# First rows' variance taken ahead of the second rows' statistics, the first weights converted on GpSimd, and transposed rows in four tiles at both ends

## The chip, the cores and the metric

The kernel runs on one core of a Trainium2 chip. The metric is the device time of one execution in microseconds. The core has five engines with queues of their own: TensorE (PE; its weight loads are PEld), VectorE (DVE), ScalarE (ACT), GpSimd (POOL) and SyncE (SP), which only issues transfers here. ACT issues transfers too. The engines run in the order of their queues and meet through semaphores.

## The reference

Two equal layers: sliding-window attention with 32 heads of 20 over 2048 rows of 640 (window 256), and a dense block with a squared ReLU; both have a layernorm ahead and a residual around them.

```
def _A_ref(x, wqkv, wo):
    B, S, D = x.shape                      # 1, 2048, 640
    H = 32; Dh = D // H; W = 256
    qkv = (lambda x, *d: x.transpose(*d))((x @ wqkv).reshape(B, S, 3, H, Dh), 2, 0, 3, 1, 4)
    q, k, v = qkv[0], qkv[1], qkv[2]
    scores = jnp.einsum("bhqd,bhkd->bhqk", q, k) * (Dh ** -0.5)
    idx = jnp.arange(S)
    mask = (idx[:, None] - idx[None, :] >= 0) & (idx[:, None] - idx[None, :] < W)
    scores = jnp.where(mask[None, None], scores, -1e9)
    p = _softmax(scores, axis=-1)
    o = jnp.einsum("bhqk,bhkd->bhqd", p, v)
    return (lambda x, *d: x.transpose(*d))(o, 0, 2, 1, 3).reshape(B, S, D) @ wo

def _B_ref(x, w1, b1, w2, b2):
    h = jnp.einsum("bsd,df->bsf", x, w1) + b1     # 640 -> 1536
    r = jnp.where(h > 0, h, 0)
    return jnp.einsum("bsf,fd->bsd", r * r, w2) + b2

x = x + _A_ref(_layernorm(x), A_wqkv, A_wo);  x = x + _B_ref(_layernorm(x), ...)   # twice
```

## The kernel before

The work is cut into 16 units u: two layers of eight groups, each of 256 rows (two tiles xt of 128 x 640). A unit goes through these stages.

- **Layernorm** (`ln_load`, `layernorm`): two statistics on DVE for each tile of 128 rows (L353), aggregate (L357) and variance (L358), the power -1/2 on GpSimd (L364), the scaling on DVE (L366).
- **Transposes** (`ln_t`, `split_t`): PE turns a tile in five matmuls (L391) into a PSUM tile bb, ACT casts it to a high half in fp16 (L377), DVE makes the low half as the difference (L378). Both halves stand in one tile yT.
- **Three-term products** (`mm3`, L327): each dense product is high x high + high x low + low x high, three matmuls for each of five chunks of the contraction, 15 for a block of 128 columns of q or k. High and low halves of the weights come from `convert`: ACT makes the high half (L259), DVE the low one (L260).
- **q, k** (`stage_qk`): evicted by ACT and DVE (L507, L510) into fp16 halves, then sent through DRAM in another layout (`leave`, L542 to L548). **v** (`stage_v`, L580).
- **Attention** in eight quads of four heads. `max_quad` computes all scores of a quad for their row maxima (L653; L668 for a layer's first group), with DVE reducing them (L633); `max_out` turns the maxima (L721, L726, L727) and `rows_out` sends them as a row qt<-mT that is a further row of the contraction (L689); `exp_quad` computes the scores again with it (L757, L765), ACT takes the exponential into pt (L779), GpSimd masks (L794, L798); `pv_quad` multiplies with v (L828), ot goes out through DRAM (o, L840, L845) and comes back in `load_o` (L904 to L914) as od.
- **Dense rest**: `stage_o` (od x wo), a layernorm, `stage_y` (transposed rows y2, again through `split_t`), `stage_f` (w1, ReLU L1003, square L1007, w2, the sum L1042 and the rows out).

Weights are loaded at the start: wq in seven pieces on SP's queue, `load_wq` (L273), wo in four on ACT's queue (L288, into w_s), w1 and w2 behind them. All stay in SBUF.

The order of the work on each engine is not left to a scheduler. A planner in the kernel keeps a clock `now` for PE and one for each other engine; `post` puts a job with an estimated cost (ns) and a priority into a list, and `pump` emits what can start by the planned clock. `flow` puts the first unit's quads between the dense work of the units ahead as soon as their planned inputs are there; `together` does it for later units. So a changed cost or a new job changes what is emitted behind it on all engines, until the plan falls back into step. `spin` (L341) emits matmuls on a constant tile into nothing: 14 at the start and 7 behind the first transposes. krow[0] (named kt in the profile) is the tile of the first keys, whose constant is set by four memsets of 128x512 (L96); mh are two tiles for the turned maxima, zeroed at L593.

In quarter units (all but a layer's first group) a maxima quad holds four row blocks w of 5 x 64 = 320 key columns, laid one behind the other over PSUM banks of 512 columns; a block that crosses a bank's end is cut into pieces, one matmul each. w stands for the pair j and half i:

```
for w in range(4):
    j, i = divmod(w, 2)
    p, at = 2 * qd + j, 5 * Q * w
    cuts = sorted({0, 5 * Q, *(z - at for z in (512, 1024) if 0 < z - at < 5 * Q)})
```

Of the kernel before, what the change touches and what calls it, by code (L numbers as in the profile page):

```python
# [11 lines left out]
F16 = mybir.dt.float16  # L12
BF16 = mybir.dt.bfloat16
AF = mybir.ActivationFunctionType
ALU = mybir.AluOpType
# [30 lines left out]
def kernel(ctx: ExitStack, tc: tile.TileContext, x, wqkv, wo, w1, b1, w2, b2, out):  # L46
# [50 lines left out]

    for k in range(4):
        set_row(0, k)

# [155 lines left out]

    def convert(st, hi, low, n, load, *deps, prio=2):

        a = post("A", 20 + 0.9 * n, lambda: nc.scalar.activation(hi, st, AF.Copy, scale=WS), load, *deps, prio=prio)  # L259
        return post("D", 30 + 1.04 * n, lambda: nc.vector.scalar_tensor_tensor(low, st, WS, hi, op0=ALU.mult,  # L260
                                                                               op1=ALU.subtract), a, prio=prio)
# [59 lines left out]

    def mm3(acc, lhs, rhs, nk, ns, then=None):

        k, t = 0, 0.0
        for c in range(nk):
            for a, b in ((0, 0), (0, 1), (1, 0)):
                nc.tensor.matmul(acc, lhs(a, c), rhs(b, c), start=(k == 0), stop=(k == 3 * nk - 1))  # L327
# [17 lines left out]

    def layernorm(src, y, *deps, prio=2):

        box = {}

        def stats(i):  # L350
            if i == 0:
                box["st"] = sb.tile([P, 2, 6], F32, name="bst", bufs=2)
            nc.vector.bn_stats(box["st"][:, i, :], src[:, i * HD:(i + 1) * HD])  # L353

        def var():
            box["mv"] = mv = sb.tile([P, 4], F32, name="bmv", bufs=2)
            nc.vector.bn_aggr(mv[:, 0:2], box["st"])  # L357
# [6 lines left out]
        j = post("G", 520, lambda: nc.gpsimd.tensor_tensor(box["mv"][:, 3:4], box["mv"][:, 2:3], neghalf,  # L364
                                                                   op=ALU.pow), j, prio=prio)
        j = post("D", 576, lambda: nc.vector.tensor_scalar(y, src, box["mv"][:, 0:1], box["mv"][:, 3:4],  # L366
                                                           op0=ALU.subtract, op1=ALU.mult), j, prio=prio)
        return j

    def split_t(y, dst, job, made, bb=None):  # L370

# [4 lines left out]
        def out(tr, jobs, c0, n, wait):  # L376
            j = post("A", 170 * n, lambda: nc.scalar.copy(dst[:, 0, c0:c0 + n], tr[:, :n]), wait=wait, prio=0)  # L377
            j = post("D", 170 * n, lambda: nc.vector.tensor_sub(dst[:, 1, c0:c0 + n], tr[:, :n], dst[:, 0, c0:c0 + n]), j,  # L378
                     prio=0)
# [32 lines left out]
    def ln_load(u, *deps, prio=2):  # L412
# [3 lines left out]
        for i in range(2):  # L416
            xt = sb.tile([P, D], F32, name="xt", tag="xt", bufs=2)
            load = dma(lambda xt=xt, i=i: nc.sync.dma_start(xt, xsrc(l, 2 * g + i)), P * D * 4, *deps, prio=min(prio, 1))
            ys.append((xt, layernorm(xt, xt, load, prio=prio)))
        lns[u] = ys  # L420

    def ln_t(u, yT=None):
        ys = lns.pop(u)
        if yT is None:
            yT = sb.tile([P, 2, KC, T], F16, name="yT", tag="yT", bufs=1)
        yTs[u], pre[u] = yT, []
        bb = banks() if u == 0 else (None, None)
        for i in range(2):
            yield from split_t(ys[i][0], yT[:, :, :, i * P:(i + 1) * P], ys[i][1], pre[u], bb[i])

# [24 lines left out]
    def ln_cross(u, *deps):  # L455
# [4 lines left out]
        def dst():  # L460
            yTs[u] = sb.tile([P, 2, KC, T], F16, name="yT", tag="yT", bufs=1)
            return yTs[u]

# [14 lines left out]
    def stage_qk(u, which=(0, 1)):  # L478
# [9 lines left out]
        for j, c0 in order:  # L488
# [33 lines left out]
            for c in range(n):  # L522
                lo = j * D + (c0 + c) * P
                need(wqj[lo // P])
                yield from mm3(acc[:, c, :], lambda a, k: wq_s[:, a, k, lo:lo + P],
                               lambda b, k: yT[:, b, k, :], KC, 109, evict if c == n - 1 else None)

# [39 lines left out]
    def stage_v(u, which=range(4)):  # L567
        yT = yTs[u]
        for i in range(2):
# [3 lines left out]
            for h in range(2):  # L573
# [5 lines left out]
                def out(vt=vt, acc=acc, h=h):  # L579
# [3 lines left out]

                yield from mm3(acc[:, :HD], lambda a, k: yT[:, a, k, i * P:(i + 1) * P],
                               lambda b, k: wq_s[:, b, k, 2 * D + h * HD:2 * D + (h + 1) * HD], KC, 136,
# [5 lines left out]
    mhs = [sb.tile([P, P], F16, name=f"mh{i}") for i in range(2)]  # L591
    for m in mhs:
        nc.vector.memset(m, 0.0)  # L593

# [12 lines left out]
    def by_tiles(pieces):  # L607
# [5 lines left out]
        for _, _, put in sorted(order, key=lambda o: o[:2]):  # L613
            for e in range(2):
                put(e)

    def max_quad(n):
# [19 lines left out]
        if quarters(u):  # L637
            flat = [b.rearrange("p a n -> p (a n)") for b in bb]
            pieces = []
            for w in range(4):  # L640
                j, i = divmod(w, 2)
                p, at = 2 * qd + j, 5 * Q * w
# [16 lines left out]
            now[0] += 763.0  # L659
            for w in range(4):  # L660
# [301 lines left out]
    def y_cross(u):  # L962
        def dst():
            y2s[u] = sb.tile([P, 2, KC, T], F16, name="y2", tag="qd", bufs=1)
            return y2s[u]

# [7 lines left out]
    def stage_y(u, *between):  # L974

        y2s[u] = y2 = sb.tile([P, 2, KC, T], F16, name="y2", tag="qd", bufs=1)
        ypre[u] = []
        bb = banks() if u == NU - 1 else (None, None)
        for i in range(2):
            y, j = ys.pop((u, i))  # L980
            yield from split_t(y, y2[:, :, :, i * P:(i + 1) * P], j, ypre[u], bb[i])
            for g in between[i:i + 1]:
                yield from g

    def stage_f(u, ahead=None):
# [8 lines left out]
        for f0 in range(0, FC, 2):  # L994
# [26 lines left out]
            for f in range(2):  # L1021
                fo = (f0 + f) * P
                need(w1j[f0 + f])
                yield from mm3(acc[:, f, :], lambda a, k: w1_s[:, a, k, fo:fo + P],
                               lambda c, k: y2[:, c, k, :], KC, 109, evict if f else None)
        if ahead is not None:
# [164 lines left out]

    spin(14)
    ln_load(0, prio=0)
    load_wq()
    run(ln_t(0))
    spin(7)
    rate[0] = 250.0
# [86 lines left out]
```

## Time and profile before

| | us |
|---|---|
| median of 3 runs | 1586.17 |
| lowest, highest | 1585.07, 1589.79 |
| the profiled execution, its own time | 1588.33 |
| its span in the trace | 1586.6 |
| granted clock of TensorE, mean over the span | 0.995 |

The span is what the profiler saw between the first and the last instruction; 1.7 us of the profiled execution's time lie around it. In the rows of a timeline the first two numbers are the start and the length in us, then come engine, line, operation, output <- inputs and a count; in brackets stand the idle time of the engine just before and what ended it. Neighbouring instructions of one kind are drawn together (x148). In the rows of windows there are the busy time and the count of each engine, then the granted clock (PEclk, 1.00 is full speed), the share of the DMA engines and GB/s. In the groups by line, the numbers behind the bar are the busy time in us and the mean ns of one.

### The profile page before, as it was taken

To read this page: it belongs to the slowest core of one execution; us is meant where nothing else is said; L and a number is where in the kernel's file an instruction comes from. 1 tells how busy PE (TensorE), PEld (TensorE's weight loads), DVE (VectorE), ACT (ScalarE), POOL (GpSimd) and SP (SyncE) were. 2 spreads that over 40 slices of the span, in tenths; PEclk is the share of its full clock that TensorE was granted. 3 is DMA by queue.
4 is the path that set the end of the run, shared out by engine and by line. 5 is a ranking of instruction groups with operands and counts; after the bars stand their busy time and mean duration, and the time that the engine had idled before them with its cause. 6 is when DMAs were issued, how large, how long until landed. Compare 5 with 4: busy or idle time off the path is not lost. (4 is left out here: it accounts for less than half of the span.)

```text
span 1586.6 us, 52541 instructions
## 1 busy us (share of the span) xinstructions
PE 1558.1 (98%) x21570; PEld 1168.7 (74%) x21570; DVE 984.7 (62%) x3254; ACT 734.3 (46%) x1593; POOL 600.3 (38%) x1291
## 2 busy tenths in 40 slices
PE   8899999999999999999999999999999999999989
PEld 7666777777777777777777777777778777676767
DVE  8776665666756656565566656657665666756532
ACT  4455545444454444535443453444535345354512
POOL 1233534235253443524324252442525325254512
PEclk9998999999999999999999999999999999999999
DMA  9764343362533525354352534535343343431020
GB/s 272 191 181 117 77 107 86 96 131 55 122 87 103 111 57 127 78 124 90 91 132 64 121 87 110 104 70 128 68 125 83 97 111 69 114 87 58 29 67 18
DMA packets 243353, 160.44 MB, mean 101 GB/s; under 512 B 91176, under 2 KB 226856, under 8 KB 243112
## 3 DMA queue, kind: packets, MB, share of 16 engines
q1 hardware_dynamic: 236744, 147.58, 38.8%
q10 hardware_dynamic: 6368, 9.50, 2.1%
q8 instruction: 169, 2.77, 0.7%
q14 instruction: 72, 0.59, 0.1%
HBM read 84.68 MB, written 52.95 MB: 87 GB/s over the span
## 5 line engine op out<-in xcount | busy, mean ns | idle before, releaser
L779 ACT ACTIVATE pt<-bb 128x512 f32<-128x512 f32 (+1 forms) x736 | 376.0, 600 | 227.0 <-PE bb L757 197.8
L633 DVE CUSTOM_DVE_ANT_0 bb<-bb,maskq 128x320 f32<-128x320 f32 x896 | 409.2, 524 | 86.8 <-PE bb L653 74.6
L794 POOL TENSOR_SCALAR_AFFINE_SELECT pt<-pt 128x256 f32<-128x256 f32 x448 | 188.0, 422 | 563.1 <-ACT pt L779 550.3
L327 PE MATMUL acc<-y,w_s 128*128 128x256 f16 x2880 | 328.3, 273 | 2.5 <-ACT y L377 1.4
L327 PE MATMUL acc<-w_s,hh 128*128 128x320 f16 (+1 forms) x2340 | 326.1, 297 | 0.0
L327 PEld LDWEIGHTS <-w_s 128*128 128x128 f16 x2880 | 276.5, 98 | 54.4 <-issue 18.1
L327 PEld LDWEIGHTS <-hh 128*128 128x128 f16 x2340 | 222.1, 98 | 96.8 <-issue 11.5
L327 PEld LDWEIGHTS <-wq_s 128*128 128x128 f16 x2400 | 229.9, 98 | 46.3 <-issue 13.5
L327 PE MATMUL acc<-yT,wq_s 128*128 128x256 f16 x2250 | 258.6, 273 | 2.2 <-DVE qd L510 0.8
L798 POOL TENSOR_SCALAR_AFFINE_SELECT pt<-pt 128x256 f32<-128x256 f32 x512 | 213.7, 439 | 93.0 <-ACT pt L779 91.6
L1013 DVE TENSOR_TENSOR hh<-r,hh 128x256 f16<-128x256 f32 x192 | 95.1, 517 | 208.8 <-ACT hh L1010 201.8
L828 PE MATMUL pv<-pt,vt 128*32 128x128 f32 (+1 forms) x3840 | 190.9, 331 | 1.2 <-POOL pt L798 1.2
L1007 POOL TENSOR_TENSOR r<-r 128x256 f32<-128x256 f32 x192 | 114.2, 615 | 161.2 <-ACT r L1003 158.8
L840 ACT COPY ot<-pv 128x256 f32<-128x256 f32 x128 | 47.7, 373 | 268.8 <-PE pv L828 268.7
L327 PE MATMUL acc<-wo_s,od 128*128 128x320 f16 x960 | 141.7, 303 | 4.8 <-ACT od L911 3.0
L633 DVE DVE_READ_ACCUMULATOR2_ANT mx<- 128x1 f32 x1024 | 145.1, 142 | 0.0
L828 PEld LDWEIGHTS pv<-pt,vt 128*32 128x32 f32 x3840 | 105.4, 110 | 41.7 <-POOL pt L798 6.5
L327 PE MATMUL acc<-wq_s,yT 128*128 128x320 f16 x900 | 132.0, 299 | 1.4 <-DVE y L378 0.9
L327 PEld LDWEIGHTS <-od 128*128 128x128 f16 x960 | 92.1, 99 | 51.0 <-issue 6.4
L1003 ACT ACTIVATE r<-acc,b1s 128x256 f32<-128x256 f32 x192 | 80.7, 472 | 87.7 <-PE acc L327 86.4
L327 PEld LDWEIGHTS <-yT 128*128 128x128 f16 x900 | 85.7, 98 | 39.3 <-issue 6.7
L364 POOL TENSOR_TENSOR bmv<-bmv,neghalf 128x1 f32<-128x1 f32 x64 | 45.5, 717 | 136.1 <-DVE bmv L358 135.7
(95 smaller groups left out, 1226.3 us busy)
## 6 DMA issues: line engine op xcount, KB each, us to landing
qt<-qk SPq DMA_DIRECT2D x30, 480.0 KB
kt<-qk SPq DMA_DIRECT2D x30, 480.0 KB
qk<-qd SPq DMA_DIRECT2D x17, 640.0 KB
o<-ot SPq DMA_DIRECT2D x256, 42.0 KB
od<-o SPq DMA_DIRECT2D x14, 640.0 KB
qk<-yl SPq DMA_DIRECT2D x13, 640.0 KB
qk<-qd SPq DMA_DIRECT2D x17, 320.0 KB
xt<-in_A_x_dram SPq DMA_DIRECT2D x16, 320.0 KB
```

The costliest lines, as they stand in the source:

```text
L327: nc.tensor.matmul(acc, lhs(a, c), rhs(b, c), start=(k == 0), stop=(k == 3 * nk - 1))
L364: j = post("G", 520, lambda: nc.gpsimd.tensor_tensor(box["mv"][:, 3:4], box["mv"][:, 2:3], neghalf, op=ALU.pow), j, prio=prio)
L633: nc.vector.tensor_tensor_reduce(out=v, in0=v, in1=mask, scale=1.0, scalar=-3.0e38, op0=ALU.add, op1=ALU.max, accum_out=accum[e, w]),
L779: nc.scalar.activation(box["pt"][:, :o], bb[e][:, k, :o], AF.Exp, scale=SCALE / (QS * QS))
L794: nc.gpsimd.affine_select(out=m, in_=m, pattern=[[0, 2], [-1, P]], compare_op=ALU.is_gt, fill=0.0, base=0, channel_multiplier=1)
L798: nc.gpsimd.affine_select(out=m, in_=m, pattern=[[0, 2], [1, P]], compare_op=ALU.is_ge, fill=0.0, base=0, channel_multiplier=-1)
L828: nc.tensor.matmul(pv[32 * jj:32 * (jj + 1), q0 * P:(q0 + qn) * P], vf[:, c:c + 32], pj[:, j, :], start=(k == 0), stop=(k == len(steps) - ...
L840: nc.scalar.copy(ot[:, qd % 2], pv)
L1003: nc.scalar.activation(box["r"], acc[:, f, :], AF.Relu, bias=b1s[:, f0 + f:f0 + f + 1], scale=1.0 / (YS * WS))
L1007: nc.gpsimd.tensor_tensor(box["r"], box["r"], box["r"], op=ALU.mult)
L1013: nc.vector.tensor_sub(hh[:, 1, f, :], box["r"], hh[:, 0, f, :])
```

## The change

Five edits.

1. `ln_load` and `layernorm`: for u = 0 the first tile's aggregate and variance are made before the second tile's statistics, and both scalings after both variances.
2. The four memsets of krow[0] and the two of mh go from DVE to GpSimd (`set_first`), posted behind the first unit's transposes.
3. The high half of the first 128 columns of wq is made by GpSimd (`tensor_scalar`) in place of ACT.
4. The transposed rows of u = 0 and u = 15 stand in four tiles in place of one (high chunks 0 to 2, high 3 and 4, low 0 to 2, low 3 and 4), so that a matmul waits for its own piece. The first q block of u = 0 and the first w1 block of u = 15 take their three terms one after the other over all five chunks (`whole`), not chunk by chunk: for u = 0 high x high, high weights x low rows, low weights x high rows; for u = 15 the last two the other way round.
5. The order of the row blocks in a maxima quad is `TURN`: (0,1), (0,0), (1,0), (1,1). With the bank ends at 512 and 1024 the pieces of one pair of heads that lay in two banks become one: 36 matmuls for a quad in place of 38, in 112 quads. The spins are 13 and 4 in place of 14 and 7.

```diff
-    for k in range(4):
-        set_row(0, k)
...
-    def convert(st, hi, low, n, load, *deps, prio=2):
-
-        a = post("A", 20 + 0.9 * n, lambda: nc.scalar.activation(hi, st, AF.Copy, scale=WS), load, *deps, prio=prio)
+    def convert(st, hi, low, n, load, *deps, prio=2, first=False):
+
+        if first:
+            a = post("G", 1400, lambda: nc.gpsimd.tensor_scalar(hi, st, WS, None, op0=ALU.mult), load, prio=0)
+        else:
+            a = post("A", 20 + 0.9 * n, lambda: nc.scalar.activation(hi, st, AF.Copy, scale=WS), load, *deps, prio=prio)
...
                 wqj[(lo + z) // P] = convert(st[:, :, z:z + P], wq_s[:, 0, :, c], wq_s[:, 1, :, c], KC * P, load,
-                                             prio=1)
+                                             prio=1, first=not lo + z)
...
+    def set_first():
+        rowset[0] = [post("G", 560, lambda k=k: nc.gpsimd.memset(krow[0][:, 512 * k:512 * (k + 1)], PAIR), prio=2)
+                     for k in range(4)]
+        for m in mhs:
+            post("G", 150, lambda m=m: nc.gpsimd.memset(m, 0.0), prio=2)
...
-    def mm3(acc, lhs, rhs, nk, ns, then=None):
+    def mm3(acc, lhs, rhs, nk, ns, then=None, whole=0):
 
         k, t = 0, 0.0
-        for c in range(nk):
-            for a, b in ((0, 0), (0, 1), (1, 0)):
+        terms = ((0, 0), (0, 1), (1, 0))
+        if whole:
+            terms = [[t] for t in (terms if whole == 1 else terms[::2] + terms[1:2])]
+        for c, part in ([(c, part) for part in terms for c in range(nk)] if whole else [(c, terms) for c in range(nk)]):
+            for a, b in part:
                 nc.tensor.matmul(acc, lhs(a, c), rhs(b, c), start=(k == 0), stop=(k == 3 * nk - 1))
...
-        j = None
+        j = behind
         for i in range(2):
             j = post("D", 455, lambda i=i: stats(i), j, *(deps[i:i + 1] or deps), prio=prio)
-        j = post("D", 400, var, j, prio=prio)
+        v = j = post("D", 400, var, j, prio=prio)
         j = post("G", 520, lambda: nc.gpsimd.tensor_tensor(box["mv"][:, 3:4], box["mv"][:, 2:3], neghalf,
                                                                    op=ALU.pow), j, prio=prio)
-        j = post("D", 576, lambda: nc.vector.tensor_scalar(y, src, box["mv"][:, 0:1], box["mv"][:, 3:4],
-                                                           op0=ALU.subtract, op1=ALU.mult), j, prio=prio)
-        return j
+        def scale(*more):
+            return post("D", 576, lambda: nc.vector.tensor_scalar(y, src, box["mv"][:, 0:1], box["mv"][:, 3:4],
+                                                                  op0=ALU.subtract, op1=ALU.mult), j, *more, prio=prio)
+
+        return scale() if first is None else (v, scale)
+
+    def pieces_of(*tiles):
+
+        return lambda a, c, n, m: tiles[2 * a + c // 3][:, c % 3:c % 3 + n, m]
...
+            behind = ys[0][1][0] if u == 0 and i else None
+            ys.append((xt, layernorm(xt, xt, load, prio=prio, behind=behind, first=True if u == 0 else None)))
+        if u == 0:
+            last = ys[1][1][0]
+            ys = [(xt, scale(last)) for xt, (v, scale) in ys]
...
+        if u == 0:
+            yT = pieces_of(sb.tile([P, 3, T], F16, name="yT", tag="yT", bufs=1), sb.tile([P, 2, T], F16, name="rs", bufs=1),
+                           *[sb.tile([P, n, T], F16, name="x1", bufs=2) for n in (3, 2)])
...
+    TURN = ((0, 1), (0, 0), (1, 0), (1, 1))
...
-            for w in range(4):
-                j, i = divmod(w, 2)
+            for w, (j, i) in enumerate(TURN):
...
-                    reduce(e, w, flat[e][:, 5 * Q * w:5 * Q * (w + 1)], maskq, 5 * Q)
+                    reduce(e, 2 * j + i, flat[e][:, 5 * Q * w:5 * Q * (w + 1)], maskq, 5 * Q)
...
+        if u == NU - 1:
+            y2 = pieces_of(sb.tile([P, 3, T], F16, name="y2", tag="qd", bufs=1), sb.tile([P, 2, T], F16, name="rs", bufs=1),
+                           sb.tile([P, 3, T], F16, name="y2", tag="yT", bufs=1), sb.tile([P, 2, T], F16, name="y2", tag="pt", bufs=6))
...
-    spin(14)
+    spin(13)
     ln_load(0, prio=0)
     load_wq()
     run(ln_t(0))
-    spin(7)
+    set_first()
+    spin(4)
```

In the changed file the lines stand some ten to thirty lower: the statistics are L363, the variance L368, the scaling L377, the low casts L400, the products L337, the value evictions L611, the loads of wo L295.

How the order moves. First the start of DVE: bst are the statistics, bmv mean and variance, kt_85 the first keys' tile. Before:

```order
L96 MEMSET kt_85 128x512 x4
L593 MEMSET mh_129 128x64
L593 MEMSET mh_130 128x64
L353 BN_STATS bst<-xt 128x6 x3
L357 BN_AGGR bmv<-bst 128x2
L358 TENSOR_SCALAR bmv<-bmv 128x1
L353 BN_STATS bst<-xt 128x6
L357 BN_AGGR bmv<-bst 128x2
L358 TENSOR_SCALAR bmv<-bmv 128x1
L366 TENSOR_SCALAR xt<-xt,bmv 128x640 x2
```

And now:

```order
L86 MEMSET vt_91 128x11
L363 BN_STATS bst<-xt 128x6 x2
L367 BN_AGGR bmv<-bst 128x2
L368 TENSOR_SCALAR bmv<-bmv 128x1
L363 BN_STATS bst<-xt 128x6 x2
L367 BN_AGGR bmv<-bst 128x2
L368 TENSOR_SCALAR bmv<-bmv 128x1
L377 TENSOR_SCALAR xt<-xt,bmv 128x640 x2
```

The first tile's aggregate and variance moved from behind the third statistics to behind the second, and the memsets are gone from the queue.

The second place is ACT's queue around the loads of wo, while the first unit's maxima go out on SP. Before:

```order
L580 ACTIVATE vt_89<-acc 128x16x20
L288 DMA w_s<-in_A_wo_dram 32x5x640
L580 ACTIVATE vt_89<-acc 128x16x20
L288 DMA w_s<-in_A_wo_dram 32x5x640
L507 ACTIVATE qd<-acc 128x2x256
L288 DMA w_s<-in_A_wo_dram 32x5x640
```

And now:

```order
L399 CAST kt_87<-tr 128x2x128
L611 ACTIVATE vt_89<-acc 128x16x20 x2
L295 DMA w_s<-in_A_wo_dram 32x5x640 x2
L537 ACTIVATE qd<-acc 128x2x256
L295 DMA w_s<-in_A_wo_dram 32x5x640
L809 ACTIVATE pt<-bb_127 128x512
```

The second load of wo moved behind the second of the two value evictions, next to the third load.

The third place is the start of the last unit's w1 blocks on PE (bb are the transposes, y the transposed rows, w_s the weights), with the semaphores waited for. Before:

```order
L391 MATMUL bb_134<-ident,xt 128x128 x4
L327 LDWEIGHTS w_s
L327 MATMUL acc<-y_27463,w_s 128x256 [waits Activation_49]
L327 LDWEIGHTS w_s
L327 MATMUL acc<-y_27463,w_s 128x256 [waits DVE_49]
```

And now (the rows left out are weight loads and matmuls from y_27238 and rs without a wait):

```order
L413 MATMUL bb_128<-ident,xt 128x128 x4
L337 LDWEIGHTS w_s
L337 MATMUL acc<-y_27238,w_s 128x256 [waits Activation_49]
...
L337 MATMUL acc<-rs,w_s 128x256 [waits Activation_49]
...
L337 MATMUL acc<-y_27240,w_s 128x256 [waits DVE_49]
```

The wait for the low rows' DVE moved from the second matmul of the block to the eleventh.

More of the change, by code (lines that the diff above doesn't have):

```diff
@@ L344, in spin, with layernorm @@
         jobs.append(free)
-    def layernorm(src, y, *deps, prio=2):
+    def layernorm(src, y, *deps, prio=2, behind=None, first=None):
         box = {}
@@ L460, in dst @@
         def dst():
-            yTs[u] = sb.tile([P, 2, KC, T], F16, name="yT", tag="yT", bufs=1)
-            return yTs[u]
+            yT = sb.tile([P, 2, KC, T], F16, name="yT", tag="yT", bufs=1)
+            yTs[u] = halves(yT)
+            return yT
         pre[u] = cross(lns.pop(u), dst, lambda: sb.tile([P, 2, 2, D], F16, name="yl", tag="qd", bufs=1), prio)
@@ L582, in out @@
                                                  AF.Copy, scale=1.0 / (YS * WS))
-                yield from mm3(acc[:, :HD], lambda a, k: yT[:, a, k, i * P:(i + 1) * P],
+                yield from mm3(acc[:, :HD], lambda a, k: yT(a, k, 1, slice(i * P, (i + 1) * P)),
                                lambda b, k: wq_s[:, b, k, 2 * D + h * HD:2 * D + (h + 1) * HD], KC, 136,
@@ L659, in max_quad @@
             now[0] += 763.0
-            for w in range(4):
+            for w, (j, i) in enumerate(TURN):
                 for e in range(2):
-                    reduce(e, w, flat[e][:, 5 * Q * w:5 * Q * (w + 1)], maskq, 5 * Q)
+                    reduce(e, 2 * j + i, flat[e][:, 5 * Q * w:5 * Q * (w + 1)], maskq, 5 * Q)
         else:
@@ L963, in dst @@
         def dst():
-            y2s[u] = sb.tile([P, 2, KC, T], F16, name="y2", tag="qd", bufs=1)
-            return y2s[u]
+            y2 = sb.tile([P, 2, KC, T], F16, name="y2", tag="qd", bufs=1)
+            y2s[u] = halves(y2)
+            return y2
         def room():
```

30 lines of the change are left out of this document (17 added, 13 removed).

## The prediction

> **What bounds the kernel now.** I read the page first, then the windows around every dip in the granted clock, then the timeline of the start, of 34 to 49 us and of the end. The page:
>
> ```profile
> span 1586.6 us, 52541 instructions
> PE 1558.1 (98%) x21570; PEld 1168.7 (74%) x21570; DVE 984.7 (62%) x3254; ACT 734.3 (46%) x1593; POOL 600.3 (38%) x1291
> PEclk9998999999999999999999999999999999999999
> ```
>
> TensorE is busy for 98% of the span. All that an edit elsewhere can give back is the 1586.6 - 1558.1 = 28.5 us in which TensorE idles, plus the time it ran at half clock. That time can be counted:
>
> ```profile
> core 0: us, PE busy (x) PEld busy (x) DVE busy (x) ACT busy (x) POOL busy (x), PEclk, DMA share, GB/s
> 4.90:12.70 7.80, 5.80 (x48) 4.82 (x47) 6.17 (x15) 4.02 (x8) 1.40 (x2) 1.00 1.03 326
> 45.50:48.90 3.40, 1.41 (x15) 1.10 (x16) 1.96 (x7) 0.67 (x2) 0.00 (x0) 1.00 0.61 131
> 48.90:52.30 3.40, 3.40 (x26) 1.89 (x28) 0.54 (x5) 0.97 (x3) 2.57 (x6) 0.50 0.63 197
> 69.40:72.80 3.40, 1.47 (x9) 0.79 (x9) 3.03 (x13) 1.78 (x5) 0.00 (x0) 1.00 0.65 198
> 72.80:76.20 3.40, 3.40 (x18) 1.70 (x18) 2.29 (x5) 1.35 (x4) 0.60 (x2) 0.50 0.99 291
> 113.80:117.20 3.40, 1.35 (x46) 0.95 (x49) 2.82 (x9) 2.26 (x5) 3.40 (x6) 1.00 0.71 226
> 117.20:127.40 10.20, 7.92 (x53) 4.19 (x43) 8.58 (x28) 2.04 (x5) 0.78 (x3) 0.50 1.12 235
> ```
>
> Three times, 3.4 us in which TensorE was busy for only 1.35 to 1.47 us (40 to 43%) are followed by stretches at clock 0.50. A 3.4 us stretch at half clock does 1.7 us of work, so each costs 1.7 us on top of the idle time ahead of it. After 127.4 us the clock stays at 1.00. So the change can act in three places: the start, the layer's ramp to 127 us, and the last stage.
>
> **Start.** Timeline, 0 to 14 us, the rows that matter:
>
> ```profile
> 1.66 2.11 DVE L96 MEMSET kt<- 128x512 f32 x4
> 4.94 0.49 DVE L353 BATCH_NORM_STATS2 bst<-xt 128x6 f32<-128x320 f32 x1 [0.28 <-DMA xt<-in_A_x_dram]
> 5.35 0.19 DVE L357 BATCH_NORM_AGGREGATE bmv<-bst 128x2 f32<-128x12 f32 x1
> 5.64 0.48 DVE L353 BATCH_NORM_STATS2 bst<-xt 128x6 f32<-128x320 f32 x1
> 6.48 0.60 DVE L366 TENSOR_SCALAR xt<-xt,bmv 128x640 f32<-128x640 f32 x1
> 7.53 0.61 DVE L366 TENSOR_SCALAR xt<-xt,bmv 128x640 f32<-128x640 f32 x1 [0.45 <-POOL bmv L364]
> 8.80 1.73 PE L341 MATMUL spin<-ident 128*128 128x128 f32 x14
> 9.04 1.03 ACT L377 CAST yT<-bb 128x256 f16<-128x256 f32 x3 [0.62 <-DVE yT L378]
> 9.95 2.64 ACT L259 ACTIVATE wq_s<-w_s 128x640 f16<-128x640 f32 x4
> 10.10 0.89 DVE L378 TENSOR_TENSOR yT<-bb,yT 128x384 f16<-128x384 f32 x2 [0.23 <-ACT yT L377]
> 10.76 0.39 PE L327 MATMUL acc<-yT,wq_s 128*128 128x256 f16 x2 [0.24 <-ACT wq_s L259]
> 10.91 1.55 DVE L260 SCALAR_TENSOR_TENSOR wq_s<-w_s,wq_s 128x640 f16<-128x640 f32 x2
> 11.78 16.33 PE L327 MATMUL acc<-yT,wq_s 128*128 128x256 f16 x148 [0.63 <-DVE wq_s L260]
> 12.75 1.36 ACT L259 ACTIVATE wq_s<-w_s 128x640 f16<-128x640 f32 x2 [0.17 <-DMA w_s<-in_A_wqkv_dram]
> ```
>
> The second row tiles land at 4.94 (DVE waits for the transfer). The memsets that leave DVE end before that, so they win nothing. What wins is the order: the first rows' aggregate and variance stand between the second rows' two statistics (5.35 to 5.64), and now fill the wait ahead of 4.94. Everything behind moves 0.3 us forward: scales at 6.2 and 7.2, casts done at 10.07 - 0.3 = 9.8.
>
> The first projection block is 15 matmuls. Now it starts at 10.76, stops after two for the low half of the weights and runs from 11.78. The spacing is 16.33/148 = 0.11 us, so it ends at 11.78 + 13 x 0.11 = 13.2, and from there TensorE never stops until 28.1 (148 matmuls in one group). Whatever this block wins is therefore won whole. After the change it needs the casts (9.8) and the high weights from GpSimd. Three pieces of the weights lie in line; the third landed at 12.75, each is 128x5x256x4 = 655 KB, at 326 GB/s 2.0 us, so the first is in at about 8.75. GpSimd's conversion (128x640) has no row. The nearest:
>
> ```profile
> 1.80 0.40 POOL L69 TENSOR_SCALAR_AFFINE_SELECT maskw<-maskw 128x256 bf16<-128x256 bf16 x1
> L959 POOL TENSOR_TENSOR x<-x,xt 128x320 f32<-128x320 f32 x60 | 51.5, 883 | 11.2 <-DMA xt<-in_B_b_dram 9.0 <-issue 2.2
> ```
>
> One operand: 0.40 x 640/256 = 1.0 us. Two operands: 2 x 0.883 = 1.77 us. The new instruction reads one tile, so it is nearer the first; writing a narrower type adds something unknown, and I take 1.3. High weights at 8.75 + 1.3 = 10.05 (9.75 to 10.5). The block starts at 10.1 with the 10 matmuls that need no low weights, which last to 11.2. Low weights on DVE: behind the low rows' casts, which end 0.3 us earlier at 10.7, plus 0.78 (half of 1.55) is 11.5; 0.3 us of stall remains. The block ends at 10.1 + 15 x 0.11 + 0.3 = 12.05: **-1.15 us** (-0.7 if GpSimd takes 1.77, -1.4 at best).
>
> The Trainium skill, "GPSIMD Engine Reference", section "4.1 Engine selection", rates GpSimd about twice as slow as VectorE with two inputs, and near line rate with one. By it the conversion would take about what DVE's 128x640 scale takes (0.60 us), TensorE would start at the casts, 9.8, but still meet the low weights at 11.5: the sum would be -1.2, nearly the same.
>
> The spins only fill waits: 7 of them are 14 passes of 0.12 us, to 10.5, ahead of a block that started at 10.76. With 4 they end at 8.5 + 8 x 0.12 = 9.5 and leave 0.6 us empty before 10.1; one fewer ahead of the transposes leaves 0.25 us. On the path they cost nothing. What the clock rows say would hurt is under 1.5 us busy in 3.4: TensorE idled 2.0 of the 7.8 us from 4.90, in at least three pieces, and still kept 1.00; the change adds 0.85 us of empty time, and takes the stop of 0.6 us and more behind the first two matmuls away.
>
> GpSimd's four key constants and two zeroed tiles come behind its conversion. By the same row four of 128x512 take 4 x 0.8 = 3.2 us, done by 14, while TensorE still has blocks until 28.1 and GpSimd does nothing from 45.50 to 48.90 (window above). Price nothing; if they ran over, the first keys' transfer would wait.
>
> **Ramp to 127 us.** The planner sees other end times and reorders every engine up to about 150 us. Two places are of consequence.
>
> ```profile
> 39.71 2.88 SPq L689 DMA_DIRECT2D qt<-mT  x4
> 41.44 0.57 ACTq L288 DMA_DIRECT2D w_s<-in_A_wo_dram  x1
> 44.72 0.57 ACTq L288 DMA_DIRECT2D w_s<-in_A_wo_dram  x1
> PE bb L765 <- DMA qt<-mT: 2.3, 2, 1.5
> 115.62 0.27 PE L653 MATMUL bb<-kt,qt 60*64 60x256 f16 x1 [1.94 <-ACT pt L779]
> 121.52 0.72 PE L327 MATMUL acc<-wo_s,od 128*128 128x320 f16 x2 [2.27 <-ACT od L911]
> ```
>
> At 45.5 TensorE waits 2.3 us for the transposed maxima's rows, and the half-clock stretch from 48.9 follows. Between their issue (39.71) and that, a transfer of output weights was issued at 41.44. In the new order the second and third such transfers stand together behind both value evictions of the second 128 rows, later relative to the maxima. The most this can give is the wait and the half clock, 2.3 + 1.7 = 4.0 us; the least is nothing, if the rows' transfer time is its own.
>
> Against it stands cover. The order shows fewer dense matmuls between the first unit's attention quads late in the ramp: 120 in place of 140 ahead of the quad at 115.62, and 5 fewer ahead of the load of the attention output awaited at 121.52. Matmuls of 0.11 us: 20 x 0.11 = 2.2 us and 0.55 us less cover for the waits of 1.94 and 2.27. Those matmuls run elsewhere in the ramp, some of them where 45.5 us is idle, so this is partly the same time moved. I take a little under 40% of the reward, **-1.5 us** net, between -4.0 and +2.75.
>
> **112 quads of maxima.** The new order of the row blocks cuts 38 matmuls to 36 in each.
>
> ```profile
> 719.56 0.76 PE L653 MATMUL bb<-kt,qt 60*64 60x256 f16 x38
> 720.25 1.51 PE L828 MATMUL pv<-pt,vt 128*32 128x256 f32 x32
> 701.88 0.75 PE L757 MATMUL bb<-qt,kt 62*64 62x192 f16 x32
> 702.57 3.16 PE L327 MATMUL acc<-wq_s,yT 128*128 128x320 f16 x22
> ```
>
> Start to next group: 720.25 - 719.56 = 0.69 us for the 38 matmuls of a maxima quad, 702.57 - 701.88 = 0.69 us for the 32 of a score quad that sends the same number of columns (four blocks of 320) through each half of the array. The count isn't paid, the columns are, and the columns stay. **-0.1 us**; were it paid by count, 0.69/38 x 2 x 112 = -4.1 us.
>
> **End.** The last unit's transposed rows in four tiles:
>
> ```profile
> 1543.35 0.27 PE L327 MATMUL acc<-y,w_s 128*128 128x256 f16 x1 [1.40 <-ACT y L377]
> 1543.60 0.89 DVE L378 TENSOR_TENSOR y<-bb,y 128x384 f16<-128x384 f32 x2 [0.23 <-ACT y L377]
> 1544.22 2.02 PE L327 MATMUL acc<-y,w_s 128*128 128x256 f16 x17 [0.60 <-DVE y L378]
> ```
>
> One matmul ran at 1543.35, the second waited until 1544.22 for the low rows. Now ten matmuls that need only high rows come first: 10 x 0.11 = 1.1 us from 1543.35 to 1544.45, when the low rows (done at 1543.60 + 0.89 = 1544.49) are there. The gap of 0.87 goes but for the first matmul's own 0.11: **-0.8 us** (0 to -0.9), and nothing behind it waits before the end.
>
> **Sum:** -1.15 - 1.5 - 0.1 - 0.8 = -3.55 us. The profiled execution took 1588.33 us (span 1586.6 and 1.7 around it), 2.16 above the median of the three runs, 1586.17. From it: 1584.8; from the median, which I use: **1582.6 us**.
>
> **Rivals.**
> 1. *The cover lost is worth more than the wait won.* Place: the quad at 115.62 and the output load at 121.52. Price: 2.75 us of lost cover, and each further 3.4 us with under 1.5 busy adds 1.7 at half clock. The other terms give -1.15 - 0.1 - 0.8 = -2.05. With the maxima's wait unchanged: -2.05 + 2.75 + 1.7 = +2.4, 1588.6; two more such stretches make it 1592.0. It decides once lost cover and half clock exceed 2.05 us. For it: 113.8 to 117.2 is already at 1.35. Against: the number of matmuls in the ramp is the same. 0.15.
> 2. *Full reward.* The maxima's rows are there in time, both the wait and the half clock after 45.5 go, and the stretch from 72.8 keeps full clock as well (1.47 busy was near the limit): -2.05 - 4.0 - 1.7 = -7.75, 1578.4. For it: the wait is the largest on TensorE in the ramp, and its neighbour in the queue moves. 0.20.
> 3. *Matmuls are paid by count.* -3.55 - 4.0 = 1578.6. The two equal 0.69 us speak against it. 0.07.
> 4. *The clock drops at the start.* The empty time at the start falls into one 3.4 us stretch with the waits around the transposes, and the first blocks run at half clock for 3.4 us: +1.7, 1584.3. The Trainium skill, "TensorE: Matmul & The Clock Gate", section "Part 1: The HAM clock gate (the "warmup" mystery)", says that the window of about 3.4 us runs freely and that an idle one throttles, which speaks against cutting spins; the trace's stretches agree in length and in halving, though they came behind 40 to 43% busy, not behind idle time alone. 0.06.
> 5. *GpSimd is the slow one.* It takes 1.77 us or more beside DVE's work, TensorE waits for it and the start gives 0.7 or less: 1583.1. 0.04.
>
> **How the numbers follow.** My forecast has 0.48. A measurement tells about 0.3%, 4.8 us, from no change: faster is under 1581.4, slower over 1590.9. Faster: nearly all of rivals 2 and 3 (0.25) and a quarter of the forecast, whose own range is 1580 to 1586 (0.12): 0.37. Slower: half of rival 1, with the further stretches at half clock, and 0.03 for the scatter of single runs (1585.07 to 1589.79 before): 0.10. The rest, 0.53, is no change. The range takes in rivals 2 and 3 downward and rival 1's first step upward: 1577 to 1588.5.
>
> **What would show it.** First block without a stop of 1 us, ending near 12.1, and GpSimd's conversion between 1.0 and 1.8 us. Windows of 3.4 us at clock 0.50: three or four where there were five. The wait of L765's matmuls for the maxima's rows under 1 us. Maxima's groups of 36 matmuls still 0.69 us to the next group. At the end, no wait behind the first matmul of the last unit's block. I am wrong if more stretches at half clock stand in the ramp than before, or if the maxima's groups shrink with their count.

## The result, and the profile after

The changed kernel is slower by 0.21%: median 1591.43 us (1587.73 to 1594.91, 16 runs) against 1587.01 us (1584.34 to 1592.43, 16 runs), ratio 1.0021 with a 95% interval of 1.0012 to 1.0030. That is 3.3 us more by the ratio (4.4 by the medians) where 3.6 us less were forecast, and it lies above the range. Of the experiments below, e12 had one run of 3982.61 us beside ten of 1580 to 1585; its ratio leaves that run out.

The page of the changed kernel, its profiled execution at 1590.61 us:

```profile
span 1588.9 us, 52082 instructions
PE 1556.1 (98%) x21338; PEld 1167.6 (73%) x21338; DVE 983.4 (62%) x3248; ACT 734.1 (46%) x1592; POOL 603.7 (38%) x1298
PEclk9999999999999999999999999999999999999999
```

TensorE is busy 2.0 us less than before in a span that is 2.3 us longer: it idles 4.3 us more. Its clock is no worse: three stretches of 3.4 us at 0.50, where the profiled execution of before had five. So the loss is waiting, and the windows of the changed kernel show where (columns as in the prediction's windows):

```profile
100.00:128.00 28.00, 20.67 (x264) 13.55 (x261) 22.99 (x68) 12.77 (x27) 6.29 (x12) 0.88 0.79 195
sum 148.00, PE 131.88 PEld 95.47 DVE 116.22 ACT 78.59 POOL 38.28; mean PE 26.38 PEld 19.09 DVE 23.24 ACT 15.72 POOL 7.66
1411.30:1414.70 3.40, 3.10 (x29) 2.64 (x27) 1.29 (x2) 2.31 (x6) 3.38 (x6) 1.00 0.29 50
1414.70:1418.10 3.40, 1.40 (x48) 1.00 (x51) 0.91 (x2) 2.77 (x7) 3.28 (x9) 1.00 0.02 4
1418.10:1421.50 3.40, 3.40 (x36) 2.11 (x29) 3.40 (x16) 0.37 (x1) 0.49 (x1) 0.51 0.05 13
```

The same stretches of before:

```profile
100.00:128.00 28.00, 22.73 (x257) 15.31 (x256) 23.69 (x69) 12.43 (x26) 7.52 (x12) 0.82 0.74 186
sum 148.00, PE 134.66 PEld 97.04 DVE 112.73 ACT 77.54 POOL 37.30; mean PE 26.93 PEld 19.41 DVE 22.55 ACT 15.51 POOL 7.46
```

From 12 to 160 us (the sums) TensorE idles 148.0 - 131.9 = 16.1 us, before 13.3. The ten profiled executions of the kernel before and of experiments that keep its plan idle 11.8 to 14.8 us there, the four with the changed plan 16.1 to 17.5. And at 1414 us, in a stage whose program is the same in both but for the order of the row blocks, it stands still, with the half clock behind it.

**Start.** The timeline of the changed kernel:

```profile
4.79 0.21 DVE L367 BATCH_NORM_AGGREGATE bmv<-bst 128x2 f32<-128x12 f32 x1
6.32 0.60 DVE L377 TENSOR_SCALAR xt<-xt,bmv 128x640 f32<-128x640 f32 x1
8.72 1.82 POOL L258 TENSOR_SCALAR wq_s<-w_s 128x640 f16<-128x640 f32 x1 [1.09 <-DMA w_s<-in_A_wqkv_dram]
10.60 0.50 PE L337 MATMUL acc<-yT,wq_s 128*128 128x256 f16 x3 [0.90 <-ACT wq_s L260]
12.03 0.38 PE L337 MATMUL acc<-rs,wq_s 128*128 128x256 f16 x2
22.02 0.49 DVE L363 BATCH_NORM_STATS2 bst<-xt 128x6 f32<-128x320 f32 x1 [1.17 <-DMA xt<-in_A_x_dram]
26.36 0.27 PE L337 MATMUL acc<-yT,wq_s 128*128 128x256 f16 x1 [0.66 <-DVE stg L540]
```

And one row of before:

```profile
25.07 0.49 DVE L353 BATCH_NORM_STATS2 bst<-xt 128x6 f32<-128x320 f32 x1
```

GpSimd's conversion took 1.82 us. The first block ran from 10.60 without a stop to 12.2 (its last two matmuls start at 12.03), against 13.2: 1.0 us won. (The row puts the stop ahead of 10.60 down to ACT's conversion of other columns; GpSimd's ended at 10.54.) At 26.36, however, TensorE waits for a low eviction on DVE (stg), in a stretch that had no stop before. DVE is late because the next rows' first statistics, at 25.07 before, now stand at 22.02, ahead of the last three low halves of the weights, and wait 1.17 us there for their load. TensorE then stands where before stood (its 150th weight load on wq starts at 27.78, before's at 27.73), and the win is gone.

**Ramp.** TensorE's waits of the changed kernel from 12 to 160 us (total, times, longest), and the groups of pv matmuls, one for each quad:

```profile
PE bb L683 <- ACT pt L809: 3.3, 3, 1.9
PE acc L337 <- ACT od L941: 2.4, 1, 2.4
PE tr L751 <- DVE x L969: 1.2, 1, 1.2
PE bb L698 <- ACT pt L809: 1.2, 1, 1.2
PE bb L795 <- DVE bmv L368: 1.0, 1, 1.0
```

```profile
76.60 1.37 PE L858 MATMUL pv<-pt,vt 128*32 128x256 f32 x16
89.69 0.86 PE L858 MATMUL pv<-pt,vt 128*32 128x256 f32 x16
```

The wait for the maxima's rows has shrunk from 2.3 us to 1.0, but is not gone: it is L795's. The list puts a wait for several semaphores down to the one that changed last, here DVE's bmv, which these matmuls do not read. The last of the four transfers qt<-mT landed at 46.29 us, and they went on at 46.43. New are 1.1 us more for L683, 1.2 for L698 and 1.2 for L751. Between the first unit's fifth and sixth pv there are 13.1 us. Before there were 6.4 (83.74 to 90.10). The same dense work stands in another distribution: less of it between the early quads, a lump in the middle, less at the end.

**Late.** The changed kernel's timeline around 1410 us:

```profile
1403.54 0.37 SPq L982 DMA_DIRECT2D xt<-in_B_b_dram  x1
1404.02 0.95 SPq L579 DMA_DIRECT2D kt<-qk  x2
1409.12 2.50 POOL L989 TENSOR_TENSOR x<-x,xt 128x320 f32<-128x320 f32 x3 [4.55 <-issue]
1411.58 1.18 POOL L1043 TENSOR_TENSOR r<-r 128x256 f32<-128x256 f32 x2
1412.23 0.41 ACT L1046 CAST hh<-r 128x256 f16<-128x256 f32 x1 [3.20 <-POOL r L1043]
1413.11 2.05 ACT L809 ACTIVATE pt<-bb 128x512 f32<-128x512 f32 x4
1416.43 0.21 PE L683 MATMUL bb<-kt,qt 60*64 60x128 f16 x1 [2.03 <-ACT pt L809]
```

And before:

```profile
1403.78 0.37 SPq L952 DMA_DIRECT2D xt<-in_B_b_dram  x1
1405.81 0.91 SPq L548 DMA_DIRECT2D kt<-qk  x2
1407.68 2.50 POOL L959 TENSOR_TENSOR x<-x,xt 128x320 f32<-128x320 f32 x3 [2.21 <-issue]
1411.66 2.05 ACT L779 ACTIVATE pt<-bb 128x512 f32<-128x512 f32 x4
```

It is read from top to bottom. The bias b2 is loaded into xt, and four additions of it stand in GpSimd's queue ahead of the squares r. Before, with the keys' transfer (two issues of 480 KB) sent 2.0 us behind the load, the load landed at 1407.55, and the additions started 3.9 us after its issue (1407.68). With the keys' transfer sent 0.5 us behind it, it landed at 1409.00, and they started after 5.6 us. Behind them the squares, ACT's casts of them, ACT's exponentials and TensorE's next maxima wait in a row.

**End.** The changed kernel's last unit:

```profile
1546.41 0.49 PE L337 MATMUL acc<-y,w_s 128*128 128x256 f16 x3 [1.40 <-ACT y L399]
1546.73 0.38 PE L337 MATMUL acc<-rs,w_s 128*128 128x256 f16 x2
1547.50 1.69 PE L337 MATMUL acc<-y,w_s 128*128 128x256 f16 x14
```

There is no stop left behind the first matmul; the 0.87 us are won.

### The profile page after: what moved, and what is told of

Read it like the earlier page. It is cut to its first block, busy times and chain, and to the rows that moved or that the text cites. A ratio compares the mean times of both kernels' runs of the same rounds, so it can differ in the third digit from the quotient of the medians.

```text
span 1588.9 us, 52082 instructions
## 1 busy us (share of the span) xinstructions
PE 1556.1 (98%) x21338; PEld 1167.6 (73%) x21338; DVE 983.4 (62%) x3248; ACT 734.1 (46%) x1592; POOL 603.7 (38%) x1298
## 5 line engine op out<-in xcount | busy, mean ns | idle before, releaser
L337 PE MATMUL acc<-y,w_s 128*128 128x256 f16 x2832 | 328.1, 273 | 1.9 <-ACT y L399 1.4
L337 PE MATMUL acc<-w_s,hh 128*128 128x320 f16 (+1 forms) x2340 | 326.1, 297 | 0.0
L337 PEld LDWEIGHTS <-w_s 128*128 128x128 f16 x2880 | 276.8, 98 | 54.5 <-issue 17.8
L337 PEld LDWEIGHTS <-hh 128*128 128x128 f16 x2340 | 222.1, 98 | 96.8 <-issue 11.5
L337 PEld LDWEIGHTS <-wq_s 128*128 128x128 f16 x2400 | 229.3, 98 | 46.9 <-issue 14.6
L337 PE MATMUL acc<-yT,wq_s 128*128 128x256 f16 x2160 | 253.4, 273 | 2.3 <-ACT wq_s L260 0.9
L337 PE MATMUL acc<-wo_s,od 128*128 128x320 f16 x960 | 140.6, 302 | 5.1 <-ACT od L941 3.1
L337 PE MATMUL acc<-wq_s,yT 128*128 128x320 f16 x864 | 128.5, 299 | 1.3 <-DVE y L400 0.8
L337 PEld LDWEIGHTS <-od 128*128 128x128 f16 x960 | 91.6, 99 | 50.9 <-issue 6.7
L337 PEld LDWEIGHTS <-yT 128*128 128x128 f16 x864 | 82.4, 98 | 38.0 <-issue 6.6
```

## The experiments

Twelve kernels, each timed against the kernel before in five rounds on the same chip (e1 to e4 on one chip, e5 to e8 on a second, e9 to e12 on a third). Theory P: the new order of the ramp costs more waiting than the start wins. Theory L: the loss at 1414 us is a race of two transfers.

| run | median us (runs) | ratio to before, 95% |
|---|---|---|
| the change | 1591.43 (16) | 1.0021 (1.0012 to 1.0030) |
| e1, start's edits alone | 1590.34 (12) | 1.0020 (1.0010 to 1.0030) |
| e2, row block order alone | 1588.84 (12) | 1.0008 (0.9998 to 1.0018) |
| e3, end alone | 1585.51 (12) | 0.9994 (0.9985 to 1.0002) |
| e4, nothing | 1586.93 (12) | 0.9998 (0.9987 to 1.0008) |
| e5, variance first alone | 1592.37 (6) | 1.0033 (1.0020 to 1.0046) |
| e6, all edits, old plan | 1588.55 (12) | 1.0009 (0.9999 to 1.0018) |
| e7, the same, old row blocks | 1585.99 (12) | 0.9993 (0.9983 to 1.0003) |
| e8, the same, ACT converts | 1585.33 (12) | 0.9990 (0.9982 to 0.9999) |
| e9, before, additions moved | 1586.42 (11) | 0.9994 (0.9986 to 1.0003) |
| e10, row blocks, additions moved | 1584.87 (11) | 0.9993 (0.9985 to 1.0002) |
| e11, the change, additions moved | 1587.01 (11) | 1.0006 (0.9998 to 1.0015) |
| e12, start and end, old plan, additions moved | 1583.39 (11) | 0.9975 (0.9966 to 0.9985) |

One ten-thousandth is 0.16 us.

**e1, e2, e3, e4: the change in three parts.** e1 is the changed kernel without these two edits:

```diff
-    TURN = ((0, 1), (0, 0), (1, 0), (1, 1))
+    TURN = ((0, 0), (0, 1), (1, 0), (1, 1))
...
-        if u == NU - 1:
+        if False:
             y2 = pieces_of(...)
...
-                               2 if u == NU - 1 and f0 + f == 0 else 0)
+                               0)
```

e2 is the kernel before with TURN alone, e3 the kernel before with the last unit's four tiles and order of terms alone, and e4 the changed file with everything undone.

> The start's edits alone (variance first, GpSimd's conversion and constants, four tiles and whole terms for u = 0, 13 and 4 spins), without the new order of row blocks and without the four tiles of u = 15. Theory P (the new plan of the ramp costs more waits than the start wins): slower than before by 3 to 5 us, 1590 to 1592, and in the trace more idle time of TensorE between 12 and 160 us than the 14 us or so of before. Rival T (the row blocks' order costs): no slower than before, 1584 to 1587.

> The kernel before with the new order of row blocks alone; the order of all engines but TensorE's maxima matmuls is that of before. Theory P: within 0.7 us of before, groups of 36 matmuls still 0.69 us to the next group. Rival T: slower by 3 us or more, with waits of the maxima's matmuls for ACT's exponentials that before does not have. Paid by count: faster by 4 us.

> The kernel before with the four tiles and whole terms of the last unit alone. Both theories: faster than before by 0.8 us (0 to 1.2), with no wait of TensorE for DVE's low rows behind the first matmul of the last unit's block. If the end loses what the trace of the changed kernel seemed to win, it is slower.

> The changed file with all edits undone by switches: every engine's order is that of before, line numbers apart. All theories: the same time as before within 0.7 us. Its single runs and their granted clocks show how much time moves with the clock alone: by theory a half-clock stretch of 3.4 us costs 1.7 us, so 0.001 of mean clock goes with 1.6 us.

The start's edits alone bring the whole loss (1.0020). The end is 1.0 us faster (0.9994), as expected, though its interval touches no change; nothing is nothing (0.9998). The row block order is between: 1.3 us slower where 0.7 at most was expected, with an interval that touches no change. Single runs with their clock support the reading that the loss is not clock: at a mean clock of 0.998, e1's six runs have a mean of 1589.7 us, and the six of before beside them 1585.6. At 0.996, twelve runs of before have 1588.3, so 0.002 of clock goes with 2.7 us, 1.35 us for 0.001 where 1.6 was expected. The rate itself is not settled: the runs of before beside e5 to e8 give 0.3 us for 0.001 between the same two clocks, those beside e9 to e12 0.6.

**e5: one dependency.** The kernel before with nothing but

```diff
-        j = None
+        j = behind
...
+            behind = ys[0][1][0] if u == 0 and i else None
```

and the two scalings behind both variances.

> The kernel before with one edit alone: the first rows' aggregate and variance ahead of the second rows' statistics (a dependency in the plan). It is the only one of the start's edits by which the plan puts other numbers of dense blocks between the first unit's quads. Theory P (the plan): slower than before by 3 to 4.5 us, 1590 to 1591.5, with 10 us or more of TensorE's idle time from 60 to 128 us where before has 8.3. Rival G (GpSimd's conversion and constants, or the split tiles, hold up other engines): the same as before within 0.7 us.

Slower by 0.33%, 5.2 us: the worst of all, and more than the 3 to 4.5 expected. Two small DVE instructions are moved by one place. By the planner's clock that shifts jobs by a few tenths of a us, and from there the plan takes the other course. The traces show that it is the change's course: between the first nine pv groups stand 30, 40, 20, 22, 78, 45, 35 and 40 records of dense matmuls in e5 as in the change, e1 and e11, and 35, 60, 20, 30, 25, 40, 55 and 45 in the ten others. Its waits from 12 to 160 us:

```profile
PE acc L340 <- ACT od L945: 3.6, 1, 3.6
PE bb L687 <- ACT pt L813: 3.2, 3, 1.9
PE bb L702 <- ACT pt L813: 2.3, 1, 2.3
```

**e6, e7, e8: the same start under the old plan.** The planner is given the old dependency; only what two of its jobs emit is exchanged, so that the instructions stand as in the change:

```diff
         lns[u] = ys
+        if u == 0:
+            v, b = seen[0][2], seen[1][0]
+            v.fn, b.fn = b.fn, v.fn
```

(`seen` holds the jobs of each layernorm: here the first tile's variance and the second's first statistics.) e7 also takes the old TURN, e8 also ACT's conversion.

> All edits of the change; only the planner is told the old dependency and cost order of the first variance, while the instructions stand in the new order at the start. Behind 60 instructions the order of VectorE, ScalarE, GpSimd and SyncE is that of before up to the last stage. Theory P: 1585 to 1586.5, that is faster than the changed kernel by 4.5 to 6 us and faster than before by 0.5 to 1.5 (the start's 0.9 and the end's 1.0, less what the new row block order costs). Rival G: 1590 or more, like the changed kernel.

> As the run with all edits and the old plan, but with the old order of row blocks in the maxima quads (38 matmuls). If the new order costs what its run alone showed (1 to 2 us): 1584 to 1585 and faster than with it by as much. If that was scatter: the same within 0.7 us. Paid by count: slower by 4.

> As the run before this one, but ScalarE converts the first weights again. GpSimd took 1.82 us for it in the changed kernel and ended at 10.54; ScalarE would start at its casts' end, 9.8, and take 0.66: the first block starts 0.1 us earlier, but ScalarE's second conversion ends 0.66 later. Both theories: the same within 0.5 us.

With the old plan and the old row blocks the loss is gone: 0.9993 against e1's 1.0020 with the start's edits under the new plan. Of that 0.0027, 0.0006 is the end's; 0.0021, 3.3 us, is left for the plan. e6 missed its 1585 to 1586.5. It differs from e7 in the row blocks alone, whose matmuls take what they took, and yet stands 2.6 us above it. Its profiled execution shows where: a stop of 3.1 us at the late place.

```profile
1414.67 0.21 PE L688 MATMUL bb<-kt,qt 60*64 60x128 f16 x1 [3.10 <-ACT pt L814]
```

The start won nothing beyond the end's share in e7. Its wait list has 1.1 us for DVE's low weights, because DVE made the second columns' low weights first: the first block goes on at 12.52, when the second of DVE's conversions has ended (12.46). e8, with ACT's conversion, is no worse.

**e9 to e12: the late additions.** In `add_b2`, for one unit:

```diff
-                               nc.gpsimd.tensor_tensor(..., op=ALU.add), load, prio=2))
+                               nc.gpsimd.tensor_tensor(..., op=ALU.add), load, prio=2,
+                               wait=LATE if u == NU - 3 else 0.0))
```

With LATE = 9000 ns the four additions stand further back in GpSimd's queue; nothing else moves. e12 is e7 with that and with 900 in place of 1400 as the conversion's planned cost, which puts the first columns' low weights first and still leaves the old plan.

> The kernel before, with GpSimd's four additions of b2 for unit 13 moved behind some of the squares and masks (they stand at the head of its queue at 1407 us, and wait there for the load of b2). All other engines keep their order. In four of five profiled executions with the old plan and the old row order nothing was lost there. Theory L (a race of b2's load with the keys' transfers makes the loss at 1414 us, in some executions of every kernel): faster than before by 0.3 to 1 us on the mean, with fewer runs above 1588. If the loss comes only with the change: the same as before within 0.5 us.

> The new order of row blocks alone, with the same additions moved. Theory L: what the new order cost in its own run (1.1 us on the mean of the runs, 1.9 us of it in the profiled one at 1414 us) goes; within 0.5 us of the kernel before with the additions moved. Rival T (the order costs in itself): it stays slower than that one by 1 us or more.

> The changed kernel with the same additions moved. Theory L: the 3.8 us that the profiled execution lost between 1405 and 1428 us go, a mean gain of 1.5 to 3 us over the changed kernel: 1588 to 1589.5. What is left over before, 1.5 to 3 us, is the ramp's plan (theory P), less the end's 1.0.

> The start's edits with the old plan and a planned 900 ns for GpSimd's conversion, so that VectorE makes the first columns' low weights first, the last unit's four tiles, the old order of row blocks, and the additions moved. Theories P and L together: the first block ends 0.8 us earlier and the low weights are no longer second in line (1.1 us of waiting in the run with all edits and the old plan), the end 1.0: faster than before by 1.5 to 2.5 us, 1584 to 1585.

Theory L holds. The change goes from 1.0021 to 1.0006, 2.4 us; the row block order from 1.0008 to 0.9993, so in itself it costs nothing; before itself by 0.0006, its interval touching no change. In all four profiled executions the pv group after 1410 us follows 10.12 us behind the one ahead of it, whether the keys' transfer was issued 0.5 us behind the bias's load (e10, e11) or 2.1 us (e12); in the executions without the edit it took 10.35 to 13.8 us. e11 and e12 came out faster than expected, by 1.0 and 0.6 us. The whole wait that is left there, in e12:

```profile
PE bb L688 <- ACT pt L814: 1.3, 2, 1.1
```

e11 against e10 leaves theory P by itself: 0.0013 with the end's win in it, so some 3 us for the new plan with the start's edits. e11 against e12, which has the same start's edits under the old plan (but 900 for 1400, and the old row blocks, which e10 shows to cost nothing), is 0.0031, 4.9 us. From 12 to 160 us, e11 and then e12:

```profile
sum 148.00, PE 131.46 PEld 95.42 DVE 118.06 ACT 78.66 POOL 39.62; mean PE 26.29 PEld 19.08 DVE 23.61 ACT 15.73 POOL 7.92
```

```profile
sum 148.00, PE 136.16 PEld 98.60 DVE 116.62 ACT 79.22 POOL 40.30; mean PE 27.23 PEld 19.72 DVE 23.32 ACT 15.84 POOL 8.06
```

16.5 us idle under the new plan, 11.8 under the old. e12 is faster than both kernels: 0.9975 (0.9966 to 0.9985), 4.0 us below before.

## Why the prediction was wrong

**The ramp, the step that failed.** The prediction set 40% of the reward at the maxima's rows against the lost cover and took -1.5. The reward was mostly one execution's. In all fourteen profiled executions TensorE waits at this place and goes on 0.14 us after the last transfer of the rows has landed, also where the list names DVE. It waits 0.6 to 1.0 us in the nine others with the old plan, 1.0 to 1.2 in the four with the new one, and 2.3 in before's alone. e9 is one of the nine:

```profile
PE bb L765 <- DMA qt<-mT: 0.9, 1, 0.9
```

None of the nine has the half-clock stretch that followed it at 48.9. So against the old plan as it ran in these nine there was no reward to win. The lost cover was real, and was rival 1's: the wait at the quad near 114 us stayed as it was (1.94), but 1.07 us came in the quad ahead of it, and the wait for the attention output, 2.3 to 2.4 with the old plan, was 2.4 in the change and 3.6 in e1, e5 and e11. The thin places between the early quads wait too (L698, 1.2 to 2.3). By the runs the new plan cost 3 to 5 us (e1 against e7, e11 against e12), where the rival priced 2.75; with what the start won it left some 3 (e11 against e10). e5 and e12 show it from both sides. Counting the matmuls between quads gave about the right number; discounting it because "those matmuls run elsewhere" was the error, since where they run decides.

**The start** was right in mechanism (1.0 us won at the first block for 1.15) and wrong in "won whole". That TensorE never stopped from 13.2 to 28.1 was a fact of the old order; the change reorders DVE in that stretch, and the statistics that wait for their load take the win back. That hangs on the load: in e1, with the same start, they waited 0.31 us for it, TensorE did not stop, and 0.6 us of the win were left (its 150th weight load at 27.13). In e12, where they stand behind the low weights again, 0.9 us were left (26.87). GpSimd's conversion lies just above the upper bound (1.82 for 1.77), not near the 1.3 taken. The Trainium skill, "GPSIMD Engine Reference", section "4.1 Engine selection", has one-input operations near line rate; DVE's scale of as many elements took 0.60, so here the measurement speaks against it.

**The row blocks** were right as to the maxima: 36 matmuls, 0.69 us to the next group as before (1428.65 to 1429.34), and no cost of their own in e10.

```profile
1428.65 0.76 PE L683 MATMUL bb<-kt,qt 60*64 60x128 f16 x36
1429.34 1.51 PE L858 MATMUL pv<-pt,vt 128*32 128x256 f32 x32
```

**The end** was right: 0.87 us of stop gone, e3 at 0.9994 (0.9985 to 1.0002).

**What was not seen** is the late race, 2.4 us of the changed kernel's time by e11, of which before loses some 1.0 too (e9, its interval touching no change). The prediction held that the change can act in three places, the start, the ramp and the last stage, and so put this one at nothing. It lies in a stage that the change leaves alone but for the row blocks' order, and no row of before's single execution showed it waiting; the 2.21 ahead of L959 were hidden. The fourteen traces show what goes with its size. Issued 2.0 to 2.4 us ahead of the keys' transfer, the bias's load landed after 3.8 to 4.0 us (five executions, before's among them); 1.1 to 1.3 us ahead, after 4.95 to 5.4 (four); 0.5 us ahead, after 5.3 to 5.8 (five). Where the additions were not moved, the pv group behind them then followed the one ahead of it after 10.35 to 10.5, 11.5 to 12.0 and 12.2 to 13.8 us. The keys' transfer leaves within 0.2 us of the landing of the transfer that writes its source (qk<-yl, the later of two). That took 4.1 us from its issue in five executions, exactly the five with the new row blocks, and 4.7 to 6.0 in the nine others. So the row blocks' order goes with the race, though it adds no work; why that transfer is shorter with it is not settled, nor whether every execution of these kernels behaves as the one recorded.

**The sum** of what the runs show, each term uncertain by one to two us: the new plan with the start's edits +3.0, the row blocks -0.2, the end -1.0, the race +1.4 beyond before's. That is +3.2 for the 3.3 measured. Rival 1's +2.4 came near it partly by luck, since 1.4 of the 3.3 us are the race's.

**The clock.** Rival 4 did not come: the first half-clock stretch of the change begins at 114 us. Ahead of its three stretches TensorE was busy for 1.19, 0.76 and, late, 1.40 of 3.4 us, below the 1.5 that the prediction took from before's rows. As a limit 1.5 does not hold: in other executions half clock followed 1.75 us busy (e3, 66.41 to 69.82) and 2.08 (e12, 64.77 to 68.18). The windows of the change:

```profile
110.85:114.26 3.41, 1.19 (x21) 0.86 (x22) 2.54 (x8) 3.34 (x8) 3.09 (x6) 1.00 0.71 219
114.26:117.67 3.41, 3.41 (x67) 2.01 (x56) 2.33 (x11) 0.98 (x2) 1.05 (x3) 0.50 1.00 297
117.67:121.09 3.42, 0.76 (x7) 0.23 (x4) 3.42 (x11) 1.23 (x3) 0.00 (x0) 1.00 1.16 197
121.09:124.50 3.41, 3.41 (x14) 1.98 (x13) 3.35 (x10) 0.92 (x2) 0.00 (x0) 0.50 1.18 198
```

## What to carry to other kernels

Where a planner sets the order, a small edit at the head is an edit of everything behind it until the plan falls back in step. Test the instruction's move and the plan's reaction apart: move the instructions under the old plan, then change the plan alone. Read a wait as a reward only if several executions have it, and when a list names an engine whose output the waiting instruction does not read, look for a transfer that landed at that moment.

## What the runs showed of the hardware

DVE's scaling takes longer beside a constant of 128x512 that GpSimd writes. Its second scaling of 128x640, 0.61 us in both kernels, took 0.92 in e7, where its first 0.43 us ran beside GpSimd's first such constant (7.44 to 7.96),

```profile
7.53 0.92 DVE L382 TENSOR_SCALAR xt<-xt,bmv 128x640 f32<-128x640 f32 x1 [0.45 <-POOL bmv L379]
...
8.08 2.04 POOL L258 TENSOR_SCALAR wq_s<-w_s 128x640 f16<-128x640 f32 x1
```

and 1.24 in e8, beside three constants:

```profile
7.46 1.24 DVE L382 TENSOR_SCALAR xt<-xt,bmv 128x640 f32<-128x640 f32 x1 [0.45 <-POOL bmv L379]
7.38 1.79 POOL L284 MEMSET kt<- 128x512 f32 x3
```

The start of GpSimd's conversion does not do this: in e1 it ran beside the scaling from 7.82, and the scaling took 0.61. The conversion itself, 1.82 us in the change, where the scaling was over, took 2.04 in e7 and 2.05 in e1. So work that is moved to GpSimd because it is idle can lengthen what it was moved away from.
